# Zero products on TensorE in an attention backward loop, later row sums on GpSimd, and an earlier weight load

## The chip, the cores and the metric

One core of one Trainium2 chip. The metric is device time in microseconds of one execution of the whole program, median of several executions. Engines are named as in the profile: PE is TensorE, DVE VectorE, ACT ScalarE, POOL GpSimd, SP SyncE (it issues transfers here). A profile is of one execution only.

## The reference

A transformer block with modulated layer norms, forward and backward: attention with 32 heads of 16 columns over 2048 rows of width 512, then an MLP of width 1792 with squared ReLU; the output and the gradients of all weights and inputs but B_x are returned. What matters here is the attention's backward part:

```python
scores = jnp.einsum('bhqd,bhkd->bhqk', q, k) * Dh ** (-0.5)
p = _softmax(scores, axis=-1)
o = jnp.einsum('bhqk,bhkd->bhqd', p, v)
...                                   # MLP, residuals, layer norms
_out, _vjp = jax.vjp(_f, ...)         # all gradients but that of B_x
_grads = _vjp(grad_out)
```

## The kernel before

The backward loop works on units: 4 heads, 128 rows of q, 512 of k. There are 512 units, in 128 blocks of four. For each unit, PE makes four scores (`s`, 32 rows of the array each), ACT four exponentials (`e`), PE and DVE the product dS (`D`, two halves), PE the sums for dK and dV (`q`). dQ needs dS transposed: SP issues a transposing transfer from SBUF to SBUF for each unit, of 128 x 2048 bf16 (512 KB). The last unit of every second block is turned on PE instead (`t`) and copied out by ACT (`T`), so 7 of 8 units go through the transfers, 448 in all. PE then multiplies (`d`), ACT evicts (`Q`).

```python
def dp_pair(u, pair):                       # token D
    if pair == 0:
        bst[u][1] = ework.tile([P, 4, 512], BF, name="dS_u", tag="dS_u", bufs=6)
    ...                                     # two products into psD
    DVE.tensor_tensor(dS_u[:, 2 * pair:2 * pair + 2, :], psD[:], E_u[:, 2 * pair:2 * pair + 2, :], ALU.mult)

def on_pe(b):
    return b % 2 == 1

def transpose_unit(u):                      # after the second D of a unit
    hg, kc, qc, qi = units[u]
    if qi == 0:
        dqt[u // 4] = tpool.tile([P, 4, 16, P], BF, name="dsT", tag="dsT")
    if qi == 3 and on_pe(u // 4):
        return
    SP.dma_start(out=dqt[u // 4][:, qi], in_=bst[u][1].rearrange("p h k -> p (h k)"), transpose=True)
...
# dq_out, at a head's end: four stores, issued by ACT
        at(cur["j"] + 6 + hq, load, dQc[hg // 2, r:r + DH, :], st["dq"][32 * hq:32 * hq + DH, :])
...
order_t = (                                 # a block beside the turns
    "s0 s1 q s2 e0 e1 D s3 D e2 s4 e3 t1 e4 q T1 D "
    "s5 s6 e5 t2 e6 s7 T2 e7 D s8 e8 D s9 e9 q q s10 "
    "s11 e10 D d1 d2 e11 Q q s12 D e12 s13 e13 q s14 D e14 "
    "s15 q q e15 ").split(), "ABCABBABACABABCA"
```

The program fixes the order of each engine's instructions (`manual_schedule`). A pair of blocks (one with turns, one plain) is the unit of the argument below; there are 64.

## Time and profile before

| | before |
|---|---|
| time, median of 3 runs | 2558.0 us |
| first backward exponential starts at | 1134.2 us |
| backward loop (first to last exponential) | 1289.8 us |
| pairs without half clock / with | 20 / 44 |
| their median length | 19.31 / 20.43 us |
| part after the loop | 135 us |

### The profile page before, as it was taken

How to read it: one execution, taken by the hardware profiler on the slowest of the kernel's cores; microseconds unless marked ns; L12 is line 12 of the kernel's file. 1: busy time of each engine (PE TensorE's matmuls, PEld its weight loads, DVE VectorE, ACT ScalarE, POOL GpSimd, SP SyncE). 2: the span in 40 equal slices, each digit the busy share in tenths (PEclk: the TensorE clock that was granted, in tenths of full speed). 3: DMA queues.
4: the chain of work that ended last, by engine and by line, in shares of the span. 5: the costliest groups of instructions: out<-in, count | busy, mean ns of one | idle time of the engine just before them, and what ended most of it. 6: DMA issues, size and time to landing. Idle time of an engine off the chain costs nothing.

```text
span 2559.2 us, 50017 instructions
## 1 busy us (share of the span) xinstructions
PE 2327.6 (91%) x18734; PEld 763.9 (30%) x18734; DVE 1814.4 (71%) x2317; ACT 2307.8 (90%) x3577; POOL 347.0 (14%) x370
## 2 busy tenths in 40 slices
PE   8898799989988998999999999999999999999899
PEld 3232223223322323532222222222222222222343
DVE  6655153464435454678998999999999998998862
ACT  7999999999989999549999999999999999999942
POOL 2000101211323141110101101011010110100100
PEclk9999999999999999998999999999999999999999
DMA  7477454356648666979999999999999999999972
GB/s 205 131 192 175 147 129 120 87 166 143 90 94 188 129 141 123 275 199 191 197 196 195 193 199 202 193 197 190 194 200 195 196 197 203 195 199 207 200 243 74
DMA packets 1227128, 447.18 MB, mean 175 GB/s; under 512 B 1103095, under 2 KB 1197751, under 8 KB 1226630
## 3 DMA queue, kind: packets, MB, share of 16 engines
q1 hardware_dynamic: 1198966, 409.14, 81.2%
q0 software_dynamic: 10944, 16.78, 4.6%
q10 hardware_dynamic: 16976, 18.07, 2.6%
q8 instruction: 147, 2.41, 0.4%
q14 instruction: 95, 0.78, 0.1%
HBM read 96.75 MB, written 73.95 MB: 67 GB/s over the span
## 4 chain that ended last, share of the span: by engine, by line
PE 45%; ACT 36%; DVE 7%; issue 7%; DMA 3%; SPq 1%; ACTq 0%; DVEq 0%; POOL 0%
ACT E_u L1601 20%; ACT ET L562 11%; PE dqacc L1673 6%; PE psS_A L1595 4%; PE psST L560 3%; ACT dsT L1744 3%; PE accVK L1646 3%; PE pm L233 3%; PE psS_C L1595 3%; PE psS_B L1595 2%; PE accVK L1655 2%; PE oacc L576 2%; PE pdh L1859 2%; PE pwq L1893 2%; PE pm L398 2%
## 5 line engine op out<-in xcount | busy, mean ns | idle before, releaser
L1615 DVE TENSOR_TENSOR dS_u<-psD_u,E_u 128x1024 bf16<-128x1024 f32 x1024 | 1187.3, 1218 | 105.4 <-PE psS_B L1595 40.8
L562 ACT ACTIVATE ET<-psST 128x1024 bf16<-128x1024 f32 x1024 | 942.6, 1278 | 33.3 <-PE psST L560 32.6
L1601 ACT ACTIVATE E_u<-psS_A 128x512 bf16<-128x512 f32 x768 | 507.9, 661 | 23.3 <-PE psD_u L1613 9.8
L1601 ACT ACTIVATE E_u<-psS_B 128x512 bf16<-128x512 f32 x768 | 503.5, 656 | 5.4 <-PE ptT L1636 1.1
L1613 PE MATMUL psD_u<-iv,ido 32*128 32x512 bf16 x2048 | 423.5, 398 | 2.2 <-DVE dS_u L1615 2.0
L560 PE MATMUL psST<-qt_sb,kt_sb 32*128 32x512 bf16 x2048 | 315.0, 387 | 52.0 <-ACT ET L562 47.6
L1601 ACT ACTIVATE E_u<-psS_C 128x512 bf16<-128x512 f32 x512 | 335.0, 654 | 1.2 <-PE psD_u L1613 0.5
L1595 PE MATMUL psS_A<-ik,iq 32*128 32x512 bf16 x768 | 304.5, 396 | 12.9 <-ACT E_u L1601 2.2
L1595 PE MATMUL psS_B<-ik,iq 32*128 32x512 bf16 x768 | 305.8, 398 | 11.4 <-ACT E_u L1601 4.0
L1646 PE MATMUL accVK<-dS_u,qz 128*32 128x512 bf16 x2048 | 226.7, 414 | 0.3 <-DVE dS_u L1615 0.2
L1595 PE MATMUL psS_C<-ik,iq 32*128 32x512 bf16 x512 | 196.2, 383 | 32.9 <-ACT dsT L1744 28.9
L1595 PEld LDWEIGHTS <-iq 32*128 32x128 bf16 x2048 | 127.6, 91 | 312.0 <-issue 298.4
L1655 PE MATMUL accVK<-E_u,dOs_tok 128*16 128x512 bf16 x2048 | 211.9, 403 | 0.0
L576 PE MATMUL oacc<-ET,vaug 128*32 128x512 bf16 x2048 | 207.5, 395 | 3.2 <-DVE ostage L580 3.2
L1691 POOL TENSOR_TENSOR dQacc<-dQacc,dqtmp 128x512 f32<-128x512 f32 x64 | 81.1, 1268 | 876.8 <-ACT dqtmp L1686 876.8
L1673 PE MATMUL dqacc<-dsT,KS_tok 128*32 128x512 bf16 x2048 | 179.8, 460 | 12.1 <-DMA dsT<-dS_u 2.7
L560 PEld LDWEIGHTS <-kt_sb 32*128 32x128 bf16 x2048 | 84.8, 91 | 340.9 <-issue 320.1
L1744 ACT ACTIVATE dsT<-ptT 128x1024 bf16<-128x1024 bf16 x128 | 148.7, 1162 | 3.3 <-PE ptT L1636 3.0
L251 DVE COPY part<-pm 128x512 f32<-128x512 f32 (+2 forms) x103 | 63.5, 616 | 115.9 <-PE pm L233 110.0
L1613 PEld LDWEIGHTS <-ido 32*128 32x128 bf16 x2048 | 107.0, 91 | 109.7 <-issue 105.3
L1646 PEld LDWEIGHTS <-qz 128*32 128x32 bf16 x2048 | 60.8, 98 | 241.6 <-issue 228.6
L1636 PE MATMUL ptT<-identb,dS_u 128*128 128x128 bf16 x1024 | 80.0, 222 | 32.8 <-ACT dsT L1744 25.9
(403 smaller groups left out, 2391.9 us busy)
## 6 DMA issues: line engine op xcount, KB each, us to landing
p_st<-part POOLq DMA_DIRECT2D x36, 256.0 KB, 5.5
kt_sb<-qkT_st SPq DMA_DIRECT2D x124, 64.0 KB
wA<-in_B_w_dram SPq DMA_DIRECT2D x28, 256.0 KB
dsT<-dS_u SPq DMA_TRANSPOSE x448
wB<-w1T_st SPq DMA_DIRECT2D x21, 256.0 KB
wA<-w2T_st SPq DMA_DIRECT2D x21, 256.0 KB
wB<-in_B_w_dram SPq DMA_DIRECT2D x21, 256.0 KB
p_st<-part POOLq DMA_DIRECT2D x25, 192.0 KB, 4.2
```

What stands on the lines that cost most here:

```text
L560: PE.matmul(ps[:, hi, :], kt_sb[r:r + 32, kt * P:(kt + 1) * P], qt_sb[r:r + 32, :], start=True, stop=True, tile_position=(r, 0))
L562: ACT.activation(ET[:, 2 * pair:2 * pair + 2, :], ps[:], AF.Exp, scale=SCALE)
L576: PE.matmul(oacc[32 * hq:32 * hq + 32, :], lhsT, ET[:, hq, :], start=(kt == 0), stop=(kt == TT - 1), tile_position=(0, 32 * hq), skip_grou ...
L1595: PE.matmul(psS[:], st["q"][r:r + 32, qt * P:(qt + 1) * P], st["k"][r:r + 32, kc * 512:kc * 512 + 512], start=True, stop=True, tile_positi ...
L1601: ACT.activation(bst[u][0][:, hq, :], sst.pop((u, hq))[:], AF.Exp, scale=SCALE)
L1613: PE.matmul(psD[:, hi, :], st["do"][r:r + 32, qt * P:(qt + 1) * P], st["v"][r:r + 32, kc * 512:kc * 512 + 512], start=True, stop=True, til ...
L1615: DVE.tensor_tensor(dS_u[:, 2 * pair:2 * pair + 2, :], psD[:], E_u[:, 2 * pair:2 * pair + 2, :], ALU.mult)
L1646: PE.matmul(cur["vk"][32 * hq:32 * hq + 32, :], hst[hg]["qz"][:, qt, hq, :], bst[u][1][:, hq, :], start=(qt == 0), stop=False, tile_positi ...
L1655: PE.matmul(acc[32 * hq:32 * hq + DH, :], dOs_tok[:, qt, (hg * 4 + hq) * DH:(hg * 4 + hq + 1) * DH], E_u[:, hq, :], start=False, stop=(qt ...
L1673: PE.matmul(acc[32 * hq:32 * hq + 32, :], KS_tok[:, kc * 4 + kt, h * DH:h * DH + 32], tT[:, :, hq * 4 + kt, :], start=(kt == 0), stop=(kt ...
L1691: POOL.tensor_tensor(dst2, dst, tmp[:], ALU.add)
L1744: ACT.activation(dst, pt[:], AF.Identity)
```

## The change

Its intent: keep PE active enough, in the windows ahead of which its granted clock fell to 0.5 (in 44 of 64 pairs), that it falls no more, with products of zeros added to the open dV/dK accumulator, two ahead of the second turn and two ahead of a later score; and take two waits out of the forward part. The core of the diff:

```diff
-            later(12, sums)
+            later(16, sums)                      # row sums on POOL
...
-            later(3, sp, dx1_st[:, ts, :], dx1_c)
+            later(5, sp, dx1_st[:, ts, :], dx1_c)
-            later(3, sp, daT..., flat(da_c), True)
-            w2_nat = load_wB(w2_src, 1, 0.67)
+            later(5, sp, daT..., flat(da_c), True)
+            w2_nat = load_wB(w2_src, 1, 0.5)     # last piece ahead of the turn
...
+        def keep_warm():
+            PE.matmul(cur["vk"][0:DH, :], KS_tok[:, 0, D:QPAD], dOs_tok[:, 0, :], start=False, stop=False,
+                      tile_position=(0, 0), skip_group_check=True)
...
-            "s5 s6 e5 t2 e6 s7 T2 e7 D s8 e8 D s9 e9 q q s10 "
+            "s5 s6 e5 f f t2 e6 s7 T2 e7 D s8 e8 D f f s9 e9 q q s10 "     # f: keep_warm()
...
+                        if b < 2 and i % 2 == 1:        # first two blocks, after every second exponential
+                            if nq > 0:
+                                keep_warm()
+                            elif nq < 0:
+                                PE.matmul(idle[:], ones_bf[:], identb.unsqueeze(1).to_broadcast([P, 4, P]), start=True, stop=True)
```

More of the change, by code (lines that the diff above doesn't have):

```diff
@@ L476, in dense_chunk @@
             dwq[0:0] = chains
-            later(3, sp, dx1_st[:, ts, :], dx1_c)
+            later(5, sp, dx1_st[:, ts, :], dx1_c)
             daT = cb.tile([P, 4, DC, P], BF, name="daT", tag="T4")
-            later(3, sp, daT.rearrange("p t o q -> p (t o) q"), flat(da_c), True)
-            w2_nat = load_wB(w2_src, 1, 0.67)
+            later(5, sp, daT.rearrange("p t o q -> p (t o) q"), flat(da_c), True)
+            w2_nat = load_wB(w2_src, 1, 0.5)
             yield 5
@@ L1715 @@
             nD, nq = -1, -4
+            idle = psx.tile([P, 512], F32, name="idle", tag="accVK")
             for b in range(NU // 4 + 3):
@@ L1739 @@
                         nq += 1
+                    elif c == "f" and 0 < nq < 2 * NU:
+                        keep_warm()
                     elif c == "t" and 0 <= b - 1 < NU // 4:
```

## The prediction

> **What bounds the kernel now.** I read four views, from coarse to fine. First the page: shares of the span, the 40 slices and their clock row.
>
> ```profile
> PE 2327.6 (91%) x18734; PEld 763.9 (30%) x18734; DVE 1814.4 (71%) x2317; ACT 2307.8 (90%) x3577; POOL 347.0 (14%) x370
> ...
> ACT  7999999999989999549999999999999999999942
> ...
> PEclk9999999999999999998999999999999999999999
> ```
>
> ACT is at 9 in nearly every slice, in the forward loop (slices 2 to 16) and in the backward loop (19 to 37): ACT is the engine to read for the bound. The clock row is printed in tenths and hides what matters: the granted clock is not evenly 0.95, it jumps between 1.0 and 0.5.
>
> Second, the view by windows, over two backward block pairs of the same code. The backward loop makes 128 blocks of 16 exponentials, in 64 pairs: a block that also turns eight-tile groups on PE ("turning"), then a plain one.
>
> ```profile
> 1883.03:1893.68 10.65, 9.30 (x103) 3.55 (x106) 9.84 (x9) 10.50 (x21) 1.27 (x1) 1.00 1.21 199
> 1893.68:1902.21 8.53, 8.23 (x78) 2.12 (x78) 8.53 (x9) 8.46 (x19) 1.27 (x1) 1.00 1.15 216
> 1943.08:1954.99 11.91, 10.75 (x103) 3.51 (x106) 10.03 (x9) 11.08 (x22) 1.27 (x1) 0.86 1.18 198
> 1954.99:1963.52 8.53, 8.23 (x78) 2.14 (x78) 8.53 (x9) 8.46 (x19) 1.27 (x1) 1.00 1.08 203
> ```
>
> Columns: length, then busy us of PE, weight loads, DVE, ACT, POOL, then the clock. In the first pair the clock is full and ACT is busy 18.96 of 19.18 us: ACT is the bound. In the second pair the turning block holds one stretch of 3.41 us at half clock, takes 11.91 instead of 10.65 us, and ACT idles 0.83 us of it. I cut the whole loop (1134.2 to 2424.0 us, 1289.8 us) into pairs by the start of every 32nd exponential and laid the clock records beside it. 20 pairs have no half-clock time (median 19.31 us), 44 have some (median 20.43 us). The half-clock stretches come every 20.48 us, six times 3.41, for ten pairs on end: a slowed pair takes almost exactly six clock windows, so the weak spot meets the same phase again. That is a resonance, and it keeps the loop slow.
>
> Third, the waits of the loop, which say who pays and where PE has room:
>
> ```profile
> PE psS_C L1595 <- ACT dsT L1744: 28.9, 61, 0.6
> PE ptT L1636 <- ACT dsT L1744: 25.9, 60, 0.4
> ACT dqtmp L1686 <- PE dqacc L1673: 25.7, 34, 2.2
> ```
>
> ACT pays at the dQ eviction (the product before it runs at half clock). PE itself idles twice per turning block, each time for an ACT eviction of turned tiles. Those two idle spots are what lowers PE's activity. Fourth, the timeline of PE there, in the full-clock pair:
>
> ```profile
> 1885.82 0.37 PE L1595 MATMUL psS_A<-ik,iq 32*128 32x512 bf16 x1
> 1886.63 0.61 PE L1636 MATMUL ptT<-identb,dS_u 128*128 128x128 bf16 x8 [0.44 <-ACT dsT L1744]
> ...
> 1887.66 0.39 PE L1613 MATMUL psD_u<-iv,ido 32*128 32x512 bf16 x2
> 1888.52 0.37 PE L1595 MATMUL psS_C<-ik,iq 32*128 32x512 bf16 x1 [0.47 <-ACT dsT L1744]
> ```
>
> In the forward loop ACT loses 29.1 us to PE in all; two spots stand out, one a late load, one POOL in DVE's way:
>
> ```profile
> PE pm L487 <- DMA wB<-in_B_w_dram: 8.1, 1, 8.1
> ACT ET L562 <- PE psST L560: 9.1, 2, 8.3
> ```
> ```profile
> 808.46 4.97 POOL L170 TENSOR_TENSOR racc<-racc,g_c 128x512 f32<-128x512 f32 x4
> 808.52 1.37 DVE L329 TENSOR_TENSOR atmp<-a_c,modbc 128x512 bf16<-128x512 bf16 x1
> 809.92 1.26 DVE L330 TENSOR_TENSOR x_c<-atmp,x_c 128x512 bf16<-128x512 bf16 x1
> ```
>
> [...] every clock record is 0.5 or 1.0 and a multiple of 3.41 us long. [...] 0.43 us DVE products take 1.37 and 1.26 us beside the POOL sums.
>
> **The change, part by part.**
>
> *Four zero products per block pair.* Each turning block gets two before the second turn and two before the psS_C score: just the two idle spots. The product adds the zero padding of KS_tok to the open accumulator, so no value changes and no new engine is waited for. Cost of one: the forward loop already has such products (L599, 16 columns by 512), and they start 0.216 us apart in the trace; after K=32 scores a K=128 product starts 0.30 us later, and scores start 0.31 us after one. First spot: last score starts 1885.82, products at 1886.12 and 1886.34, array free for the turn between 1886.55 and 1886.65, while the turn starts at 1886.63 anyway. Second: 1887.66, products at 1887.96 and 1888.18, score possible at 1888.49; it starts at 1888.52. So the price is 0 to 0.05 us per pair.
>
> *What they buy.* For each 3.41 us window of the loop I took the union of array streaming time from the matmul starts [...]. The 42 windows ahead of a drop have a median of 1.70 us (90% below 1.76); the windows that keep the clock have a median of 2.36, and 95% are above 1.93. So the limit lies near half the window. Sliding a window over ten warm pairs, the minimum is 1.58 us; with 0.43 us added in each of the two spots it is 2.16. Without counting transposes, the drops sit at 1.2 to 1.3 and the minimum goes from 1.09 to 1.53 to 1.65. Either way the weak window leaves the danger zone. That zero data counts as activity I take from the forward loop: there a unit of 1.87 us carries two such products, the windows have 1.92 to 1.97 us with them, 1.15 without, and stay at full clock.
>
> *Idle products in two blocks.* The first two pairs carry 27.3 us of half clock and take 20.38 and 22.04 us. Eight products per block add about 0.6 us to each window; the first window has 0.77 us, so it may still drop. I give it 1.5 us.
>
> *Sum for the loop.* Pairs 3 to 63 at 19.26 (mean of the warm ones, 19.18 and 19.34 alternating) plus 0.03, except one with a single other delay (20.5 without any slow clock): 60 x 19.29 = 1157.4; plus 20.5, the first two 20.2 and 20.5, the last 19.6: 1238.2 us. Gain 1289.8 - 1238.2 = 51.6 us.
>
> *Last chunk loads ahead of the turn.* In the DMA queue the last four w2 pieces stand behind the daT transpose, whose issue takes 5.92 us (719.56 to 725.5); they are issued from 725.5 and PE waits until 731.9. Now all seven stand before it and come some 6 us sooner: of ACT's 8.3 us some 7 go; the first chunk's wait on the same tile (9.4 - 8.1 = 1.3 us) goes too. Together 8 us. The daT user comes four row groups later, so its two units of delay are hidden.
>
> *Row sums at 16.* The four POOL sums (4.97 us) move 4 x 1.87 = 7.5 us later, from beside the residual products, for whose end PE waits 2.61 us and ACT 3.4 us in chunk 3, to beside the small rstd steps, where DVE has 4 to 6 us in hand (it waits 6.6 us for PE after them). Gain 3 us.
>
> **Rivals.** *The zero products turn into the wait*: in-order PE would carry 4 x 0.216 = 0.86 us per pair, 55 us in all, and eat the gain: 2550 us. For it: the turn's ACT eviction starts only 0.03 us after the turn ends, so there is no slack behind the spot. Against: both spots are as long as the pair of products. *The clock still drops*, because the gate weighs rows or columns and 16 columns count little: the loop keeps its 44 slow pairs, and the products cost double there: 2550 to 2560. Against: the forward loop. *Another engine takes over*: DVE's products start 1.14 us apart, 16 per pair, 18.2 us of 19.3; five warm pairs in a row (2205 to 2301 us) run at 19.18 to 19.34 with no new wait, DMA transposes included. So 19.26 holds, but nothing below it.
>
> **Range and chances.** 2558.0 - 51.6 - 8 - 3 = 2495.4; I say 2497, since small costs are likelier than bonuses. High end 2512: a price of 0.15 us per pair (9 us) and half the forward gain lost (6). Low end 2486: the start fully warm and the pad of rare delays gone. The 2% line is 2506.9 us, 10 above my value. Faster 0.80, within 2% 0.19, slower 0.01.
>
> **What would show it.** Right: granted clock about 0.99 in the loop, half-clock stretches there fewer than five after the first two pairs, pairs at 19.2 to 19.35 us, turning blocks at 10.7, the two PE waits on dsT near nothing, the L487 wait under 2 us, the L329 and L330 products at 0.43 us. Wrong: half clock every 20.48 us as before (the limit is not union activity), or full clock with pairs above 19.6 and ACT idle before dsT (the products are in the way), or the w2 wait at another tile.

In the trace of the kernel before the granted clock is 1.0 or 0.5 in all 114 records; 113 of them are multiples of 3.413 us long (the last, 1.29 us, ends with the trace), and all begin on one grid of that step, to within 2 ns. "Window" is one step of this grid. At full clock the starts of products of 512 columns stand 0.215 us apart, those of transposes 0.055; streaming times taken again with these have a median of 1.75 us ahead of a drop and 2.38 us where the clock is kept (1.70 and 2.36 above). "The gate" is the author's word for what lowers the granted clock: the traces show that clock and PE's work, and which work counts is the author's estimate from them.

## More of the kernel before

All runs in this study are of the state "fast".

The prediction shows the rows of PE, ACT and the clock. Two more rows of the page of the kernel before matter, DVE and the transfers, each digit a tenth of a slice of 64 us; the last lines are two transfer queues, with packets, MB and the time of their packets as a share of 16 transfer engines.

```profile
DVE  6655153464435454678998999999999998998862
...
DMA  7477454356648666979999999999999999999972
...
q1 hardware_dynamic: 1198966, 409.14, 81.2%
...
q10 hardware_dynamic: 16976, 18.07, 2.6%
```

Through the whole backward loop (slices 19 to 38) the transfer engines stand at 9, as ACT does, and as DVE nearly does. Queue q1 carries the transposes, among other transfers.

## The result, and the profile after

The kernel after took 2540.6 us, median of 4 runs (2535.8 to 2543.9), against 2557.7 us of the kernel before beside it: ratio 0.9933, 95% interval 0.991 to 0.9956. Ratios here are the mean time of one kernel's fast runs over that of the other's in the same rounds, so not quite the ratio of the medians quoted. The change helps by 17 us, where some 61 were expected; the time lies outside the predicted range.

| | before | predicted | after |
|---|---|---|---|
| first backward exponential | 1134.2 | 1123.2 | 1122.5 |
| backward loop | 1289.8 | 1238.2 | 1276.7 |
| pairs without half clock | 20 | 61 or so | 49 |
| their mean length | 19.32 | 19.29 | 19.32 |
| pairs with half clock, median | 20.43 | | 22.44 |

The forward gain is there. The clock is repaired in most pairs, and a repaired pair has the predicted length. But the loop gained 13 us, not 52: of the other 15 pairs eight took 22.4 to 24.4 us, two more than a typical slow pair before. From the page of the kernel after:

```profile
PE 2353.2 (93%) x19005; PEld 777.5 (31%) x19005; DVE 1808.8 (71%) x2317; ACT 2305.1 (91%) x3577; POOL 348.5 (14%) x370
...
ACT  7999999999999999549999999999999998998952
PEclk9999999999999999999899999999999999999999
DMA  6477454366649765979999999999999999999972
```

ACT now has slices at 8 in the loop; the transfers are still at 9 in every slice of it. The view by windows shows three blocks with turns (columns as in the prediction): a good one, one with a clock drop, one at a head's end.

```profile
1841.41:1852.20 10.79, 10.48 (x107) 3.74 (x110) 10.14 (x9) 10.79 (x22) 1.27 (x1) 1.00 1.17 208
...
1619.90:1635.42 15.52, 11.53 (x107) 3.87 (x110) 10.18 (x10) 10.64 (x20) 0.00 (x0) 0.89 1.15 201
...
1345.24:1357.16 11.92, 11.51 (x107) 3.85 (x110) 9.81 (x9) 10.82 (x20) 1.81 (x2) 0.86 1.20 204
```

In the good one ACT is busy for all 10.79 us, and PE for 10.48: the products fit, with little to spare. In the second line ACT does the same 10.64 us of work in 15.52. What ACT waits for most in the loop, from 1140 to 2390 us (engine, line, releaser: total us, times, longest):

```profile
ACT E_u L1601 <- DMA dsT<-dS_u: 9.9, 3, 3.5
ACT dsT L1756 <- PE ptT L1640: 7.5, 9, 1.2
ACT dqtmp L1690 <- PE dqacc L1677: 5.7, 14, 3.0
ACT E_u L1601 <- PE psD_u L1613: 3.7, 8, 0.9
```

Before, the largest of these was the third, over 24 us, the half-clock product ahead of the dQ eviction; it has nearly gone. The first line is new and odd: an exponential waits for a transposing transfer, whose data it does not use. The timeline of pair 25 tells how:

```profile
1622.62 12.73 SPq L1628 DMA_TRANSPOSE dsT<-dS_u  x4
...
1624.53 0.33 ACTq L1577 DMA_DIRECT2D dQc<-dQst  x1
...
1629.49 0.31 ACTq L1577 DMA_DIRECT2D dQc<-dQst  x1
1629.84 0.60 ACT L1601 ACTIVATE E_u<-psS_C 128x512 bf16<-128x512 f32 x1 [3.51 <-DMA dsT<-dS_u]
...
1630.49 1.90 PE L1677 MATMUL dqacc<-dsT,KS_tok 128*32 128x512 bf16 x16 [3.71 <-ACT E_u L1601]
```

ACT issues the dQ stores of a finished head in its own in-order stream. The store at 1629.49 uses the same completion semaphore (number 105 of the packed trace, in both) as a transpose that SP issued at 1622.62 and that landed at 1629.47; it waits for that one, and so does the exponential behind it. Then PE idles, and the clock drops at 1630.22. Three such stalls (pairs 25, 41, 49) cost 14.5 us with their drops.

The second wait belongs to drops at another place: seven pairs (5, 9 to 12, 16, 51) drop 1.67 to 1.88 us after their start, ahead of the first turn, 1.2 us each. At the place that the change mends (5.5 to 6.6 us after a pair's start) there is no drop left. The rest of the loss lies in the first two pairs (41.9 us, against 42.4 before), in pair 4, and in pairs 29, 59 and 60 (22.7 to 23.1 us), where transposes land late.

So there were three suspects: drops at the second place, semaphores, late transposes. The third I put to the trace by counting: the n-th transpose belongs to the n-th dS unit that goes that way, so the end of DVE's second half can be set beside the issue and the landing.

```
kernel after    unit   0: dS written 1126.09, issued 1126.15 to 1128.08, landed 1130.41
                unit 296: dS written 1865.31, issued 1869.27 to 1871.17, landed 1873.72
                unit 297: dS written 1867.93, issued 1871.26 to 1873.85, landed 1876.51
                unit 298: dS written 1870.66, issued 1873.94 to 1876.96, landed 1880.19
```

At the loop's start a transpose is issued as soon as its data is written. At unit 296, in a run of good pairs, it is issued 4 us later: SP is still at the one before. In the kernel after 425 of 448 transposes found their data ready before SP turned to them, and these follow each other at 2.83 us (512 KB each, some 185 GB/s). That is a mean of two cases: 2.67 us where no other transfer was issued shortly before or beside them, 2.88 us beside ACT's loads for the next head and its stores. In the backlog a pair's seven take 18.9 us without and 20.0 us with such company, so only with it are they slower than ACT, which needs 19.3. The list of waits hides this: it names DVE's dS_u as what SP waited for, in the kernel before and after alike, as the last event that it knows of. 448 x 2.83 us is 1268 us of the loop's 1277. That became the theory: **the repaired loop is paced by the transposes** (with what runs beside them), and the stalls are where their backlog comes through. The rivals: the drops and the semaphores are causes of their own, each worth its own time.

### The profile page after: what moved, and what is told of

Same layout as the page of the kernel before. It is cut to its first block, busy times and chain, and to the rows that moved or that the text cites. A ratio compares the mean times of both kernels' runs of the same rounds, so it can differ in the third digit from the quotient of the medians.

```text
span 2533.7 us, 50560 instructions
## 1 busy us (share of the span) xinstructions
PE 2353.2 (93%) x19005; PEld 777.5 (31%) x19005; DVE 1808.8 (71%) x2317; ACT 2305.1 (91%) x3577; POOL 348.5 (14%) x370
## 3 DMA queue, kind: packets, MB, share of 16 engines
q1 hardware_dynamic: 1198966, 409.14, 81.9%
## 4 chain that ended last, share of the span: by engine, by line
PE 41%; ACT 37%; DVE 7%; issue 7%; DMA 5%; SPq 2%; ACTq 0%; POOL 0%; DVEq 0%; POOLq 0%
ACT E_u L1601 23%; ACT ET L562 11%; PE dqacc L1677 5%; PE psST L560 4%; PE psS_A L1595 3%; PE pm L233 3%; DMA dsT<-dS_u 2%; PE accVK L1650 2%; PE oacc L576 2%; PE psS_B L1595 2%; ACT dsT L1756 2%; PE pdh L1871 2%; PE psS_C L1595 2%; SPq L178 2%; PE pm L412 2%
## 5 line engine op out<-in xcount | busy, mean ns | idle before, releaser
L562 ACT ACTIVATE ET<-psST 128x1024 bf16<-128x1024 f32 x1024 | 942.7, 1240 | 23.4 <-PE psST L560 22.7
L1613 PE MATMUL psD_u<-iv,ido 32*128 32x512 bf16 x2048 | 412.0, 390 | 5.4 <-DVE dS_u L1615 5.2
L1595 PE MATMUL psS_A<-ik,iq 32*128 32x512 bf16 x768 | 296.2, 386 | 11.2 <-ACT E_u L1601 1.1
L1595 PE MATMUL psS_B<-ik,iq 32*128 32x512 bf16 x768 | 297.1, 387 | 9.4 <-ACT E_u L1601 1.9
L1650 PE MATMUL accVK<-dS_u,qz 128*32 128x512 bf16 x2048 | 215.4, 392 | 0.9 <-DVE dS_u L1615 0.6
L1659 PE MATMUL accVK<-E_u,dOs_tok 128*16 128x512 bf16 x2048 | 204.6, 388 | 0.0
L1677 PE MATMUL dqacc<-dsT,KS_tok 128*32 128x512 bf16 x2048 | 150.1, 392 | 25.2 <-ACT E_u L1601 10.9
L576 PEld LDWEIGHTS <-vaug 128*32 128x32 bf16 x2048 | 53.0, 93 | 122.2 <-issue 122.2
```

What stands on the lines that cost most here:

```text
L562: ACT.activation(ET[:, 2 * pair:2 * pair + 2, :], ps[:], AF.Exp, scale=SCALE)
L576: PE.matmul(oacc[32 * hq:32 * hq + 32, :], lhsT, ET[:, hq, :], start=(kt == 0), stop=(kt == TT - 1), tile_position=(0, 32 * hq), skip_grou ...
L1595: PE.matmul(psS[:], st["q"][r:r + 32, qt * P:(qt + 1) * P], st["k"][r:r + 32, kc * 512:kc * 512 + 512], start=True, stop=True, tile_positi ...
L1613: PE.matmul(psD[:, hi, :], st["do"][r:r + 32, qt * P:(qt + 1) * P], st["v"][r:r + 32, kc * 512:kc * 512 + 512], start=True, stop=True, til ...
L1650: PE.matmul(cur["vk"][32 * hq:32 * hq + 32, :], hst[hg]["qz"][:, qt, hq, :], bst[u][1][:, hq, :], start=(qt == 0), stop=False, tile_positi ...
L1659: PE.matmul(acc[32 * hq:32 * hq + DH, :], dOs_tok[:, qt, (hg * 4 + hq) * DH:(hg * 4 + hq + 1) * DH], E_u[:, hq, :], start=False, stop=(qt ...
```

## The experiments

All ratios are against the kernel before in the same rounds; "loop" is first to last backward exponential of the profiled run.

| run | kernel | median us | ratio | loop us |
|---|---|---|---|---|
| | after | 2540.6 | 0.9933 | 1276.7 |
| e1_fwd | before, forward edits only | 2556.5 | 0.9977 | 1294.9 |
| e2_prod | after without forward edits | 2551.9 | 0.9962 | 1279.6 |
| e4_spotB | after, fifth product | 2541.4 | 0.9919 | 1280.5 |
| e5_poolq | after, dQ stores from POOL | 2541.7 | 0.9922 | 1277.6 |
| e9_halfT | after, half transposes | 2504.5 | 0.9790 | 1249.1 |
| e10_halfTB | the same, fifth product | 2493.4 | 0.9746 | 1237.3 |
| c1_beforeHalfT | before, half transposes | 2550.3 | 0.9969 | 1295.6 |
| e11_turn | after, fifth product, 9 more turns on PE | 2548.8 | 0.9950 | 1294.9 |
| e3h_rows32 | half transposes, 32-row products | 2528.3 | 0.9853 | 1273.8 |
| e14_noidle | e10_halfTB without idle products | 2489.9 | 0.9714 | 1235.2 |
| e13_split | after, fifth product, split transposes | 2620.8 | 1.0228 | 1356.6 |
| e15_late | after, fifth product, loads later | 2544.7 | 0.9928 | 1274.1 |
| e16_merge | merged transposes, 3 double buffers | 2528.1 | 0.9867 | 1265.9 |
| e18_merge4 | the same, 4 double buffers | 2506.2 | 0.9772 | 1241.8 |
| e17_noidle | single transposes, no idle products | 2545.1 | 0.9927 | 1275.4 |
| e19_buf8 | the same, 8 buffers | 2543.0 | 0.9920 | 1277.5 |
| e20_after4 | after, merged, 4 double buffers, no more | 2519.6 | 0.9827 | 1248.6 |

### The two halves of the change

e1_fwd is the kernel before with the five forward lines of the diff; e2_prod is the kernel after without them.

> The kernel before with the forward edits alone (row sums lagged by 16, the two stores lagged by 5, the w2 load ahead of its turn), the backward loop untouched. Theory: the two parts are independent, and the two traces put 11.7 us of gain ahead of the first backward exponential (1134.21 to 1122.50 us); so about 2546 us against 2557.7, ratio 0.9955, and a backward loop of 1290 us with 44 or so half-clock pairs as before. Rival: the later start of the loop moves it against the clock windows and the loop changes by itself by more than 3 us; then the forward part does not explain the difference alone.

> The kernel after without its forward edits: zero products and idle products alone. Theory: the loop takes about 1277 us as in the kernel after, some 13 us under before's 1290, so about 2545 us, ratio 0.995, with about 15 pairs at half clock and the store stalls at heads' ends still there. Rival (the prediction's own sum): the loop gains 51.6 us once its phase against the clock windows is another one: 2506 us. Rival: the residual losses depend on phase and scatter, then between 2520 and 2550.

The loop of e2_prod took 1279.6 us, within 3 us of the kernel after, at another start (1134.5 us): the small gain is no accident of one phase. The total gained less than its text said (2551.9 us where it had 2545). e1_fwd's loop began 9 us earlier and was 5 us longer by its own drops (52 cold pairs, that is, pairs with half clock), the rival's case; its 4 us in the total are within the noise (interval 0.9951 to 1.0002). Over all profiles, the loop starts at 1134.2 to 1135.5 us in the three kernels without the forward edits, and at 1120.4 to 1132.0 us, 1126.2 on average, in the sixteen with them. The forward edits are thus worth 8.5 us on average, with a spread of 12 us among the sixteen.

### One suspect at a time: the drops, the stores

e4_spotB adds a product ahead of the first turn; e5_poolq moves the stores to POOL.

```diff
 e4_spotB
-            "s0 s1 q s2 e0 e1 D s3 D e2 s4 e3 t1 e4 q T1 D "
+            "s0 s1 q s2 e0 e1 D s3 D e2 s4 e3 f t1 e4 q T1 D "
 e5_poolq
-                    at(cur["j"] + 6 + hq, load, dQc[...], ...)
+                    at(cur["j"] + 6 + hq, pload, dQc[...], ...)     # pload: POOL.dma_start
```

> The kernel after with a fifth zero product per pair, ahead of the first transposes to ptT, where the clock still dropped in 7 pairs (drop 1.67 to 1.88 us after the pair's start). Theory: the gate counts array time weighted by rows, over the window's 3.41 us; the weakest window rises from 1.19 us (under the threshold of 1.28 us that both traces fit) to 1.33 us, so no drop at that place, and about 8 us less than after: 2532 us, 0.990 of before. Rival: activity is counted as the union of streaming time regardless of rows, 2.3 us in those windows already, and the drops there come from something else: then the drops stay and the time stays at 2541 us. Rival: the product delays the transposes by 0.2 us per pair and costs 64 x 0.2 = 13 us: 2550 us.

> The kernel after with the dQ stores at the end of each head issued by GpSimd in place of ScalarE. Theory: ScalarE's three long stalls (3.51, 2.88 and 3.47 us, each ending with a transfer of dsT that has nothing to do with the stalled store) come from the store waiting in ScalarE's in-order stream for a semaphore shared with the transposes' queue; without it they and the clock drops after them vanish, some 10 to 14 us: 2528 us, 0.988 of before. Rival: the transposes are late by themselves and the wait moves to the transposed tile's consumer or to VectorE's next dS tile in the same pairs: then under 3 us are gained. Rival: other transfers issued by ScalarE (the loads for the next head) meet the same wait: then half of it comes back.

Both edits did what they were made for, and neither brought anything. In e4_spotB no pair drops at 1.6 to 1.9 us; in e5_poolq no store stalls. But the totals stayed at 2541 us and the loops at 1280.5 and 1277.6 us, because the loss reappears elsewhere. ACT's waits in the loop of e5_poolq:

```profile
ACT E_u L1604 <- PE psD_u L1616: 7.4, 16, 0.9
ACT dsT L1759 <- PE ptT L1643: 6.1, 7, 0.9
ACT E_u L1604 <- PE psS_C L1598: 5.6, 10, 1.7
ACT dqtmp L1693 <- PE dqacc L1680: 4.4, 6, 3.7
```

ACT waits for the scores (psS_C) and for PE's products that DVE reads (psD_u) more than it did; other transfers of ACT met the semaphore wait (2.6 us at once, in pair 26). And the transposes ran later still behind their data: landing after writing had a median of 7.3 us in the kernel before, 8.6 in the one after, 9.3 in e4_spotB, 10.3 in e5_poolq. A loss that moves when its place is mended, with the total fixed, is the sign of a bound elsewhere.

### The decisive test: half the bytes

Each transpose moves two heads of four; the dQ products read those two twice. dQ is wrong (relative error 0.58 in that output); all instructions keep number and shape but the transposes.

```diff
-            SP.dma_start(out=dqt[u // 4][:, qi], in_=bst[u][1].rearrange("p h k -> p (h k)"), transpose=True)
+            SP.dma_start(out=dqt[u // 4][:, qi, 0:8], in_=bst[u][1][:, 0:2, :].rearrange("p h k -> p (h k)"), transpose=True)
...
-                         ... tT[:, :, hq * 4 + kt, :],
+                         ... tT[:, :, hq % 2 * 4 + kt, :],
```

> The kernel after with every dsT<-dS_u transpose made half as large (two heads of four; dQ is wrong on purpose, the matmuls keep their number and size). Theory: the loop of the kernel after is paced by the transposes on SyncE's queue. 425 of their 448 issues there found their data ready, follow each other at 2.83 us, and 448 x 2.83 is 1268 us of a loop of 1277 us; the prediction let this queue pass as hidden. With half the bytes the backlog is gone, the stalls at heads' ends (10 us) and the late pairs (29, 59, 60) too, only the drops ahead of ptT and the first pairs stay: loop about 1248 us, total about 2512 us, 0.982 of before. Rival: the queue costs a fixed time for each transpose whatever its size: 2541 us. Rival: the stalls are a matter of the shared semaphores alone: then they stay at 3 us each.

> The same half transposes, and a fifth zero product ahead of the first transposes to ptT (which alone gained nothing measurable beside the kernel after, though the drops at that place vanished). Theory: with the queue out of the way the product is worth its 8 us: about 2503 us, 0.979 of before, all pairs but the first two or three at full clock. Rival: the drops are worth nothing, as that run said: the same time as the half transposes without it.

> The control: the kernel before with the half transposes. Theory: its loop is paced by ScalarE with the half-clock stretch of 1.1 us in most pairs, 20.43 us a pair against 7 x 2.81 = 19.7 us of transposes, so the queue is hidden there: less than 6 us gained, 2552 to 2558 us, some 44 to 52 pairs still at half clock. Rival: the queue paces the loop before as well: 20 us and more gained, 2535 us.

From the page of e9_halfT, clock and transfers:

```profile
PEclk9999999999999999999999999999999999999999
DMA  7477465356648765975566566665665556556572
```

The transfers fall from 9 to 5 and 6 (q1's time from 81.9% to 53.1% of the engines' span), and 36 us come with it: 2504.5 us. In the profiles, 34 us apart, 27.6 lie in the loop, as the text said (1249.1 us where it had 1248). Another 6.1 lie behind it, which it had not: the last transpose lands 1.5 us after the last exponential and not 7.9, and the part after the loop takes 128.5 us in place of 134.6. The transposes land 1.95 us after their data, median, and no store stalls. What is left in e9_halfT are the first two pairs and ten drops at 1.67 to 1.86 us. With the fifth product these go too (e14_noidle, e16_merge and e18_merge4, which also have it, keep one such drop each): in e10_halfTB 63 of 64 pairs are at full clock, mean 19.27 us, and the loop takes 1237.3 us, where the prediction had 1238.2 (the first two pairs take 1.5 us more than it gave them, the rest a little less). ACT's waits there, from 1150 us on, all but two lines of 0.2 us:

```profile
ACT dqtmp L1690 <- PE dqacc L1677: 2.0, 13, 0.2
ACT E_u L1601 <- PE psS_C L1595: 0.7, 1, 0.7
ACT E_u L1601 <- PE psS_A L1595: 0.3, 1, 0.3
```

So the fifth product, worth nothing in e4_spotB, is worth 11 us here. The control c1_beforeHalfT has 52 cold pairs and a loop of 1295.6 us: in the kernel before the transposes paced the loop hardly or not at all, for its cold pairs have a median of 20.42 us with half transposes and 20.43 with whole ones. Its ratio of 0.9969 is 8 us where the theory allowed 6. The profiles show 6.8 us after the loop, a part that takes 128.5 us in place of 135.3: the last transpose lands 1.6 us behind the last exponential in place of 8.6. (The profiled execution was the slowest of six, so its loop may be a little long.) The bound moved with the change: with whole transposes it is worth 17 us, with half ones 46 (2504.5 against 2550.3 us, in the same rounds).

One thing the test does not separate: half transposes halve the bytes, the packets and the time that SP takes to issue one (median 2.67 us whole, 1.23 us half). Which of these sets the pace is not shown; nor does any run move ACT's loads for the next head away from the transposes.

### Which measure of PE's activity fits the drops

The prediction measured PE's activity as streaming time, whatever the rows. The drops at the second place contradict it: those windows have 2.3 to 2.5 us of it, more than many that keep the clock. I looked for a measure that fits: array time weighted by rows (in it a 32-row product counts a quarter, a transpose or a zero product of 128 rows in full, of whatever number of columns; windows of 2.3 us by one measure can so be 1.2 by the other). With a limit of 1.28 us in a window of 3.41 us it misses no drop of the two traces' loops and makes one false one in some 660 windows; with transposes left out it misses 11 or more. This is an estimate, fitted to these two traces. It was made again, more simply (some 0.21 us per 512 columns, at most the whole array at a time, windows shifted by 0.08 us): 4 windows of 677 are on the wrong side of 1.28 us. With the 0.215 us of the trace, 0.055 for a transpose and windows begun 0.06 us earlier it is 5; at the best limit and shift for each, the row measure has 4 wrong (limit 1.30 us), streaming time 17, the row measure without transposes 27, and one weighted by rows and columns 23. e3h_rows32 puts it to the test, with one product over 32 rows at each place in place of two over 128:

```diff
-  PE.matmul(..., KS_tok[:, 0, D:QPAD], dOs_tok[:, 0, :], ...)            and "f f"
+  PE.matmul(..., KS_tok[0:32, 0, D:QPAD], dOs_tok[0:32, 0, :], ...)      and "f"
```

> The kernel after with half transposes (so that the queue does not disturb) and, at each of the two places, one zero product over 32 rows in place of two over 128: 32 rows, 16 columns. Theory: the gate counts array time by rows, a product over 32 rows a quarter; at the first two places the weakest windows then lie under the threshold of 1.28 us again, so drops come back 5.7 to 6.1 us after a pair's start, where the kernel after with half transposes has none, beside those at 1.67 to 1.9; once there, pairs of 20.4 us keep them there: 15 to 45 cold pairs against 11, 2510 to 2540 us against 2504. Rival (the prediction's measure, streaming time whatever the rows): the weakest windows stay at 2.0 us, over its own threshold of 1.93, so no drop at 5.7 to 6.1 us and 2504 us.

19 pairs drop at 5.79 to 6.01 us after their start, where e9_halfT has none. The loop is 24.7 us longer, 7.7 of it in the first two pairs, whose products had 32 rows too. The drops are back where the row measure puts them. The test changes rows and number together, so alone it would leave a streaming measure with a slightly higher limit; but that one cannot have the windows of 2.3 to 2.5 us that dropped. More traces say the same. Over the loops of six of them (both kernels, e1_fwd, c1_beforeHalfT, e9_halfT, e3h_rows32: 2004 windows at full clock, 191 of them ahead of half clock) the remade row measure (with some 0.21 us) and that same limit has 14 windows wrong. At the best limit and shift for each, streaming time has 64 wrong, the row measure without transposes 81, and one weighted by rows and columns 73.

### The idle products of the first blocks

> Half transposes and the fifth zero product, without the idle and zero products of the first two blocks. Theory: those buy nothing; the first two pairs took 42.2 us with them and 40.7 us in the kernel before's loop of the same start (forward edits alone), so 0 to 1.5 us faster than the same kernel with them: 2492 to 2493 us. Rival (the prediction): they spare 1.5 us, 2495 us. The profile's first two pairs decide it rather than the total.

> A correct kernel: the one after with the fifth zero product and without the idle and zero products of the first two blocks, transposes as in the kernel after. Theory: the first pair is 4 us shorter, as with half transposes, but the queue still needs 448 x 2.85 us, so that most of it is lost in the queue: 2538 to 2541 us, 0.991. Rival: the 4 us stay in the total: 2537 us or less, 0.990. These lie near each other; the number of stalls and the loop's length in the profile are the finer sign.

The first two blocks with and without idle products, from the windows of e10_halfTB and e14_noidle (pair 0 of each):

```profile
1131.99:1155.10 23.11, 21.43 (x128) 5.12 (x128) 17.21 (x15) 17.25 (x33) 8.35 (x5) 0.78 0.50 101
```
```profile
1120.38:1138.88 18.50, 14.59 (x109) 3.53 (x108) 16.17 (x15) 16.52 (x32) 8.34 (x5) 0.82 0.64 117
```

With them PE is busy 21.43 of 23.11 us and becomes the bound of the pair; the clock is as low as without. The first two pairs take 41.9 to 42.3 us in every kernel with products of 128 rows there, 37.8 to 42.5 us without. The idle products shorten the second pair (19.1 to 19.3 us in place of 19.3 to 22.1) and lengthen the first (22.6 to 23.2 in place of 18.4 to 20.5): together they bought nothing, and cost up to 4 us where the phase was kind. In e17_noidle it was not (42.1 us), so this run tells nothing of the total, as its text feared; 441 of its 448 transposes were issued late, 2.85 us apart, which is again the loop's 1275.4 us.

### Correct kernels against the queue

First three attempts to unload the queue, or to cut it finer, with a right result:

> A correct kernel that takes load off the queue: the kernel after with the fifth zero product, and the last unit of 9 more of the 128 blocks transposed by TensorE and copied by ScalarE, as every second block already does, in place of the queue's transpose. Theory: the queue needs (448 - 9) x 2.85 = 1251 us, ScalarE 64 x 19.26 + 9 x 2.2 = 1252 us; so a loop of about 1257 us with its start, total about 2521 us, 0.986 of before, faster than the kernel after. Rival: the loop is paced by ScalarE alone and its stalls come with their own cause: 9 x 2.2 = 20 us slower than the kernel after, 2561 us.

> A correct kernel: the one after with the fifth zero product, each transpose issued as two halves, each as soon as VectorE has written its half. Theory: the queue's rate is one of bytes, 5.4 to 5.7 us for two full ones whatever the cut, so the backlog stays and the time is that of the whole transposes with the fifth product, 2541 us (0.992). Rival 1: a cost per transfer bounds it, then twice the issues make it slower, over 2600 us. Rival 2: whole transposes waste time between each other and halves overlap better: faster, down to 2500 us, and this is then the best kernel.

> A correct kernel: the one after with the fifth zero product, with three of the five large loads (0.5 MB each) that are issued on the transposes' queue in the last head moved to the end of the loop, and the other two further apart. Theory: [...] the late pairs 58 to 60, 22 us each in two traces, lose their excess of some 6 us, and the loads are still in time for the last part: 2535 us, 0.9895. Rival: the last part of the kernel then waits for them and gives it back: 2541 us or more.

e11_turn (`on_pe` true for nine more blocks) missed: two turning blocks in a row take 22.3 us, 3 us over a normal pair, not 2.2, and the clock drops in the next pair four times (21.6 to 22.8 us). (Its profiled execution was the slowest, 16 us over the median.) e13_split (each transpose as two halves, issued as each half is written) was 2620.8 us, its first rival's case: 896 halves in a loop of 1356.6 us are 1.51 us each, so two halves cost 0.17 us more than one whole. ACT's waits show the queue at work:

```profile
ACT E_u L1601 <- DMA dsT<-dS_u: 45.0, 21, 4.0
```

e15_late (three of five loads of 512 KB, on SP's queue in the last head, moved to the loop's end) took pairs 57 to 63 from 142.0 to 137.4 us (some 1.5 us a load, an estimate from these two), and gave back more in the part after the loop, which took 143 us in place of 135: the rival's case.

The figure from e13_split, an estimate from its 1.51 us a half and the 2.85 us of a whole: 0.17 us for a transfer and 2.68 us for a unit's bytes. Then fewer, larger transfers should help. e16_merge and e18_merge4 give two neighbouring units one dS tile and one transfer, four transfers a pair in place of seven; both have the fifth product and no idle products. The control e19_buf8 has single transposes with the same space, e20_after4 is the kernel after with nothing but the merging and the space.

```diff
-                bst[u][1] = ework.tile([P, 4, 512], BF, name="dS_u", tag="dS_u", bufs=6)
+                if u % 2 == 0:
+                    held["two"] = ework.tile([P, 8, 512], BF, name="dS_u", tag="dS_u", bufs=3)   # e18_merge4: 4
+                bst[u][1] = held["two"][:, 4 * (u % 2):4 * (u % 2) + 4, :]
...
+            if qi == 0 or (qi == 2 and not on_pe(u // 4)) or ...: return
+            # qi 2 before a turn: alone, as before; else:
+                SP.dma_start(out=dqt[u // 4][:, qi - 1:qi + 1].rearrange("p u t k -> p (u t) k"),
+                             in_=held["two"].rearrange("p h k -> p (h k)"), transpose=True)
```

> A correct kernel: the one after with the fifth zero product, without idle products, and with the transposes of two neighbouring units in one transfer (four transfers a pair of blocks in place of seven, the same bytes; three dS buffers of double size in place of six). Theory: 0.17 us for each transfer and 2.68 us for the bytes of one unit give 4 x 0.17 + 7 x 2.68 = 19.4 us a pair against 19.95, ScalarE needs 19.26: loop about 1250 us with a few late pairs, total about 2515 us, 0.983 of before, faster than the kernel after by 25 us. Rival 1: the rate is by bytes alone: no gain, 2541 us. Rival 2: a transfer of two units starts only when both are written and lands later, so its consumers or the dS buffers wait: slower than 2541 us.

> As the merged transposes, with four double dS buffers in place of three. Theory: if the buffers are what the merged transposes wait for, this is faster than with three, by the sum of VectorE's waits for transfers there; if the queue's rate decides, the same time as with three within 5 us.

> The kernel after with the fifth zero product, without idle products, single transposes as before, eight dS buffers in place of six. Theory: the queue's rate is the bound, so buffers only let the backlog grow longer before it blocks something: 2538 to 2546 us, 0.991 to 0.993, as with six buffers (2545 us); stalls on shared semaphores stay. Rival: the space made the merged kernel fast: 2510 us, 0.98.

> The kernel after with merged transposes and four double dS buffers, nothing else changed. Theory: the change is then worth what the half transposes showed, with the drops ahead of ptT left in: the merged kernel with the fifth product at 2506 us plus some 8 us for those drops and 3 us for the idle products: 2513 to 2518 us, 0.981 of before, 25 us under the kernel after. Rival: without the fifth product the residual drops give the queue the time it lacks: 2506 us again.

e18_merge4 is right in all outputs and takes 2506.2 us, 0.9772 of before: it beats both kernels. e16_merge missed its 2515 us by 13. The loop of e18_merge4, 1241.8 us, is within 5 us of that with half transposes. In backlog a double transfer took some 5.4 to 5.5 us (1 MB, some 192 GB/s) and a single one 2.7, so a pair needs 19.0 to 19.2 us of the queue, just under ACT's 19.27. With three buffers (2528.1 us) DVE waited for transfers to free a tile, 9.2 us in all; with four 0.2 us of it are left. The line with three:

```profile
DVE dS_u L1617 <- DMA dsT<-dS_u: 9.2, 13, 2.7
```

So the first reading of that run's text holds in kind: at three, the buffers were the wait. In size it does not: the total fell by 22 us, and the text had said the sum of these waits, 9.2; what else DVE's lateness cost is not worked out. The buffers matter only once the rate suffices, though: single transposes with eight buffers stayed at 2543.0 us. e20_after4 has the change and the merging, nothing else: 2519.6 us, 0.9827, just over the range of its text, with four drops at the second place (1.67 to 1.80 us after a pair's start) and the slow first pair still in it. The kernel before with merged transposes was not run, so how this divides between the two is not shown; c1_beforeHalfT says that the unloading alone was worth little.

## Why the prediction was wrong

- **The bound of a good pair and the weak place: right.** ACT bounds a good pair, and the resonance of 20.43 us pairs with the clock was what the products cured: no drop is left at 5.5 to 6.6 us.
- **The price of the products: right.** Good pairs have a mean of 19.32 us, as before; with five products and no other trouble 19.27.
- **"Another engine takes over ... DMA transposes included. So 19.26 holds": this step failed.** It was argued from five good pairs in a row without a new wait, 2205 to 2301 us. They are pairs 53 to 57, at the end of the last head but one and the start of the last. After pair 53 ACT loads almost nothing more for a next head, and there the landing of a transpose behind the last exponential of its unit even fell, from 9.2 us in pair 53 to 8.2 in pair 56; only in pair 57, when SP's own loads began, was it 12.3. So these pairs could not show the lack. In the kernel after, over pairs of which most have those loads beside them, it grew from 7.8 us in pair 16 to 12.6 us in pair 23, all of them at full clock from pair 17 on, and in pair 25 the first long stall came: a backlog fills first. The rate was in the trace of the kernel before: 387 of its 448 transposes were issued late, 2.81 us apart, 7 x 2.81 = 19.7 us a pair. That is less than the slow pair's 20.43 us and more than the wanted 19.26. There too it grew at full clock, from 7.2 us in pair 16 to 10.3 in pair 18, and fell from 11.1 in pair 20 to 7.1 in pair 24, all of them slow. The term mis-sized is the loop: 1276.7 us in place of 1238.2; half transposes and the fifth product gave 1237.3. The transposes' queue, which the prediction let pass as hidden, was the wait.
- **"Union of array streaming time" as the measure: wrong, of small effect here.** It fits the drops worse than array time weighted by rows (64 windows of 2004 wrong against 14), and it led me to hold the place ahead of the first turn for safe; where the queue does not hide it, that costs 11 to 12 us (e10_halfTB against e9_halfT). The rival that rows or columns weigh was thus half right by this fit: the four products of 16 columns left no drop at their place, and weighing by rows and columns fits worse (73 windows wrong against 14).
- **Idle products, 1.5 us of gain: wrong.** They gained nothing, and cost up to 4 us.
- **Forward edits, 11 us: about right**, 11.7 in the first trace, 8.5 on average. With starts that spread over 12 us, the near agreement of 11.7 is partly luck. PE's wait for w2 fell from 8.1 to 2.4 us, a little above the 2 named. The DVE products beside the row sums were to come back to 0.43 us; the mean of the L329 ones only fell from 0.63 to 0.60, so the 3 us for the sums are not shown.
- **The chances** followed from a sum whose terms were each tested on a few good pairs, so the range held only their small errors and no change of the bound.

## What to carry to other kernels

When a change takes idle time out of a loop, work out the rate of everything else that the loop needs, transfers first: pieces per round times spacing in backlog, against the new length of the round. Take that spacing where everything runs that shares the way (here 2.88 us beside other loads, 2.67 without). A few rounds without a wait prove nothing where buffers hold a backlog or where the other loads are missing; compare when data was written with when its transfer was issued. And if mending a stall leaves the total where it was, stop mending stalls and look for the rate.
